# Fixed program order on SyncE and GpSimd for the second part of a fused attention and MoE kernel

## The chip, the cores and the metric

One core of a Trainium2 chip runs the program. Five engines work side by side, each through its own instructions in order: TensorE (PE in the profile; PEld is its weight load), VectorE (DVE), ScalarE (ACT), GpSimd (POOL) and SyncE (SP), which computes nothing here and issues DMAs. GpSimd both computes and issues DMAs. An instruction waits on semaphores, and everything behind it on its engine waits with it. The metric is the time of one execution on the device in microseconds, as the median of several runs.

## What is computed

Eight batches of eight heads, 576 positions, head size 64. Attention looks back over a window of 128 positions, with a bias that falls with distance (ALiBi). Its output, laid out as 4608 tokens of 512, goes through two dense layers with a Swish between them.

```python
def _attn_ref(q, k, v):                       # (8, 8, 576, 64), float32
    scores = scale * np.matmul(q, k.transpose(0, 1, 3, 2))
    mask = (rel >= 0) & (rel < 128)
    scores = np.where(mask, scores + slopes * -np.abs(rel), -1000000000.0)
    attn = np.exp(scores - max); attn = attn / (sum + 1e-09)
    return np.matmul(attn, v)
...
x = attn_out.transpose(0, 2, 1, 3).reshape(4608, 512)
h = x @ w_in                                  # (512, 2048)
g = h * (1.0 / (1.0 + np.exp(-beta * h)))
return g @ w_out                              # (2048, 512)
```

## The kernel before

**Tiles and stages.** A batch has 5 blocks of positions (4 of 128 and one of 64: `NQB = 5`, `ROWS`). Tokens are taken 512 at a time through the dense layers: 9 groups (`NTG`), so a batch is 1.125 groups. `XT` holds the transposed attention output of three groups as a ring.

The steps of attention for batch b:

- Loads of q and k. For batches 0 to 2 by pairs of heads (`load_pair`, L109, `load_tail`), for batches 3 to 7 by blocks (`load_qk`): SyncE loads float32 rows into an `fst` buffer (13 of them; line 95 in `load_rows`), GpSimd casts them to bfloat16 into a `bst` buffer (8 of them; line 126).
- Loads of v (`load_v`). For batches 0 to 2 a SyncE load into `fst` and a GpSimd cast (line 137); for batches 3 to 7 one DMA issued from GpSimd that casts on the way (line 132). There are two `VS` buffers, used by turns.
- Transposes of q and k into `qkT` (two buffers, by turns). For batches 0 to 2 on PE (`TP`, `TT`), for batches 3 to 7 by two DMA transposes per block issued from SyncE (`TD`, line 245), ten in a batch.
- `SC(b, m, p)`: scores of a pair of heads for one half of the key blocks (PE, line 273), exponentials (ACT, line 286) and a mask (DVE, line 290). `sps`, its PSUM tile, is single from batch 2 on.
- `PV(b, qb, g)`: weights times v for one block and four heads (PE, lines 313 and 317), a reciprocal and a multiplication on DVE (lines 322 and 323) that write `xn`.
- `X(b, qb)`: `xn` transposed into `XT`. For batches 0 to 2 on PE; for batches 3 to 7 a DMA transpose issued from SyncE (line 337).

The steps of the dense layers for token group g:

- `HS(g, j)`, j from 0 to 15: four matmuls 128x128 by 128x512 (line 358), tanh on ACT (line 363), one DVE operation (line 364). It reads all of the group's `XT`.
- `OS(g, i, n)`: four matmuls of the second layer (line 374). After every fourth `OS`, ACT writes an `osb` tile (6 buffers, line 380), and a DMA stores it (line 382): issued from GpSimd, for the last group from SyncE.

**Order.** PE's order is written out by hand (`manual_schedule` for PE): `spread` deals a list of attention steps between the dense steps, called items here. H group 1 is pure: 16 `HS` with no attention between them. Then group 1 (`os(0)` and half of `os(1)` with batch 2's attention, 24 items), group 2 (`hs(2)` and the rest of `os(1)`, 24 items), and groups 3 to 8 (`hs(g)` and `os(g - 1)` by turns, 32 items), each with the attention up to the last `X` that the next group's `HS` reads (`end`). For group 2 that is X of batch 3, block 2.

The order on SyncE, GpSimd, ACT and DVE is not the program's: a scheduler sets it when the program is built, from priorities and its own estimate of when an instruction can start. `ahead` only deals loads, casts and DMA transposes of the next batch among the attention steps in the program's text. On the chip each engine then keeps the scheduler's order.

Of the kernel before, what the change touches and what calls it, by code (L numbers as in the profile page):

```python
# [11 lines left out]
BF16 = mybir.dt.bfloat16  # L12
F32 = mybir.dt.float32
P = 128
# [3 lines left out]
def kernel(  # L18
# [10 lines left out]
    nc = tc.nc  # L29
    B, H, S, D = q.shape  # L30
# [8 lines left out]
    NTE = 3  # L39
    LA = 4  # L40
    LM = P * LA
    NQB = 5
    ROWS = [P, P, P, P, 64]
    NDM = DM // P
    NFF = DFF // P
    TOKG = 512
    NTG = T // TOKG
# [8 lines left out]
    NPE = 2  # L56
# [35 lines left out]
    def load_rows(src, b, sb):  # L92
        rows = ROWS[sb]
        f = fst_pool.tile([P, H, D], F32, name="fst", tag="fst")
        nc.sync.dma_start(  # L95
            out=f[0:rows],
            in_=src[b, :, P * sb : P * sb + rows, :].rearrange("h p d -> p h d"),
        )
        return f[0:rows]
# [21 lines left out]
            )  # L121

    def load_qk(b, sb):
        t = bst_pool.tile([P, 2, H, D], BF16, name="bst", tag="bst")
        for i, src in enumerate((q, k)):
            c = nc.gpsimd.tensor_copy(out=t[0 : ROWS[sb], i], in_=load_rows(src, b, sb))  # L126
        staged[b, sb] = t
        return c

    def load_v(b, sb):  # L130
        if b >= NTE:
            nc.gpsimd.dma_start(  # L132
                out=VS[b % 2][0 : ROWS[sb], sb, :, 0:D],
                in_=v[b, :, P * sb : P * sb + ROWS[sb], :].rearrange("h p d -> p h d"),
            )
            return
        return nc.gpsimd.tensor_copy(
            out=VS[b % 2][0 : ROWS[sb], sb, :, 0:D], in_=load_rows(v, b, sb)
        )
# [102 lines left out]
    def TD(b, sb):  # L242
        src = staged.pop((b, sb))
        for i in range(2):
            nc.sync.dma_start_transpose(  # L245
                out=QK[b % 2][:, i, :, P * sb : P * sb + ROWS[sb]],
                in_=src[0 : ROWS[sb], i].rearrange("r h d -> r (h d)"),
            )
# [119 lines left out]
    def OS(g, i, n):  # L368
        gT = gts[g]
        if n == 0:  # L370
            opss[g, i] = psum_o.tile([P, DM], F32, name="ops", tag="ops")
        ops_ = opss[g, i]
        for j in range(4 * n, 4 * n + 4):
            nc.tensor.matmul(  # L374
                ops_[:], lhsT=gT[:, j, i * P : i * P + P], rhs=W2[:, j, :],
                start=(j == 0), stop=(j == NFF - 1),
            )
        if n == 3:
            osb = osb_pool.tile([P, DM], F32, name="osb", tag="osb")
            nc.scalar.mul(osb[:], ops_[:], 0.5)  # L380
            row0 = g * TOKG + i * P
            (nc.sync if g == NTG - 1 else nc.gpsimd).dma_start(out=out[row0 : row0 + P, :], in_=osb[:])  # L382


    def spread(moe, todo, lead=0, tail=3):
        done, n = 0, len(moe)
        for i, it in enumerate(moe):
            it()
            to = len(todo) * (i + 1 - lead) // (n - lead - tail)
            while done < min(len(todo), to):  # L390
                todo[done]()
                done += 1

    def sc(b, m, p):
        return lambda: SC(b, m, p)

    def pv(b, qb, g):
        return lambda: PV(b, qb, g)

    def x(b, qb):  # L400
        f = lambda: X(b, qb)
        at[b, qb] = f
        return f

    at = {}


    def ahead(b, m, r):
        td = [lambda c=c, sb=sb: TD(c, sb) for c, sb in (
            ((b, 3), (b, 4)) if m == 0 else ((b + 1, 0), (b + 1, 1), (b + 1, 2)))]  # L410
        qk = [lambda sb=sb: load_qk(b + 1, sb) for sb in ((0, 1, 2), (3, 4))[m]]
        vs = [lambda sb=sb: load_v(b + m, sb) for sb in ((2, 3, 4), (0, 1))[m]]
        ops = vs if m == 0 else []
        if b + 1 < B:
            ops = td + (vs + qk if m == 0 else qk + vs)
        elif m == 0:
            ops = td + vs
        n, k, out = len(r), 0, []
        for i, f in enumerate(r):
            out.append(f)  # L420
            while k < len(ops) and k * n <= i * len(ops):
                out.append(ops[k])
                k += 1
        return out + ops[k:]

    def by_pair(b):
        return [
            lambda: TP(b, 0), lambda: TP(b, 1), sc(b, 0, 0), lambda: TT(b), sc(b, 0, 1),
            lambda: TP(b, 2), sc(b, 1, 0), lambda: TP(b, 3), sc(b, 1, 1), pv(b, 0, 0), sc(b, 0, 2),
            pv(b, 1, 0), sc(b, 1, 2), pv(b, 2, 0), sc(b, 0, 3), pv(b, 3, 0), sc(b, 1, 3),  # L430
            pv(b, 4, 0), pv(b, 0, 1), pv(b, 1, 1), x(b, 0), pv(b, 2, 1), x(b, 1), pv(b, 3, 1),
            x(b, 2), pv(b, 4, 1), x(b, 3), x(b, 4),
        ]

    def by_block(b):

        e = b - 1
        r = [pv(e, 2, 1), pv(e, 3, 1), x(e, 2), sc(b, 0, 0), x(e, 3), pv(e, 4, 1), sc(b, 0, 1),
             x(e, 4)] if e >= NTE else [sc(b, 0, 0), sc(b, 0, 1)]
        r += [sc(b, 0, 2), pv(b, 0, 0), sc(b, 0, 3), pv(b, 1, 0)]  # L440
        t = [
            pv(b, 0, 1), sc(b, 1, 0), x(b, 0), pv(b, 1, 1), sc(b, 1, 1), x(b, 1),
            sc(b, 1, 2), pv(b, 2, 0), sc(b, 1, 3), pv(b, 3, 0), pv(b, 4, 0),
        ]
        return ahead(b, 0, r) + ahead(b, 1, t)

    with tc.manual_schedule(engines={mybir.EngineType.PE}):

# [64 lines left out]
        def hs(g):  # L513
            return [lambda j=j: HS(g, j) for j in range(NFF)]

        def os(g):
            return [lambda n=n: OS(g, n // 4, n % 4) for n in range(NFF)]


        spread(hs(0), by_pair(1), 3, 0)  # L520
        for sb in range(NQB):
            load_v(2, sb)
        for sb in (0, 1, 2):
            load_qk(3, sb)
        for it in hs(1):
            it()
        for f in ahead(2, 1, [lambda: None]):
            f()
        o1 = os(1)
        spread(os(0) + o1[0:8], by_pair(2))  # L530
        todo = sum((by_block(b) for b in range(NTE, B)), [])
        todo += [pv(B - 1, 2, 1), pv(B - 1, 3, 1), x(B - 1, 2), pv(B - 1, 4, 1), x(B - 1, 3),
                 x(B - 1, 4)]
        done = 0
        for g in range(2, NTG):
            moe = hs(g)
            if g == 2:
                moe = sum((moe[2 * n : 2 * n + 2] + [o1[8 + n]] for n in range(8)), [])
            else:
                moe = sum(([a, c] for a, c in zip(moe, os(g - 1))), [])  # L540
            end = len(todo)
            if g + 1 < NTG:
                b, r = divmod(TOKG * (g + 2) - 1, S)
                end = todo.index(at[b, r // P]) + 1
            spread(moe, todo[done:end], 0, 3 if g == 2 else 6)
            done = end
        for it in os(NTG - 1):
            it()


# [28 lines left out]
```

## Time and profile before

| | |
|---|---|
| median of 3 runs | 381.88 us (381.2 to 382.83) |
| profiled execution, whole | 382.14 us |
| profiled execution, span from first to last instruction | 380.3 us |
| PE busy | 322.1 us, 85% |
| ACT busy | 211.1 us, 56% |
| DVE busy | 195.0 us, 51% |
| GpSimd busy | 105.2 us, 28% |
| HBM read and written | 36.71 and 9.44 MB |

Times in the rows are microseconds from the span's start unless marked ns. "SPq" is SyncE's queue, which issues DMAs; a DMA's "landing" is the time from its issue to the arrival of its data. Idle time of an engine stands with the releaser that ended it. The clock column tells the granted clock of PE as a share of 2.4 GHz.

### The profile page before, as it was taken

How to read it: one execution, taken by the hardware profiler on the slowest of the kernel's cores; microseconds unless marked ns; L12 is line 12 of the kernel's file. 1: busy time of each engine (PE TensorE's matmuls, PEld its weight loads, DVE VectorE, ACT ScalarE, POOL GpSimd, SP SyncE). 2: the span in 40 equal slices, each digit the busy share in tenths (PEclk: the TensorE clock that was granted, in tenths of full speed). 3: DMA queues.
4: the chain of work that ended last, by engine and by line, in shares of the span. 5: the costliest groups of instructions: out<-in, count | busy, mean ns of one | idle time of the engine just before them, and what ended most of it. 6: DMA issues, size and time to landing. Idle time of an engine off the chain costs nothing.

```text
span 380.3 us, 6165 instructions
## 1 busy us (share of the span) xinstructions
PE 322.1 (85%) x2236; PEld 153.4 (40%) x2279; DVE 195.0 (51%) x421; ACT 211.1 (56%) x407; POOL 105.2 (28%) x173
## 2 busy tenths in 40 slices
PE   6988988998989900019999999999998999999996
PEld 2454454444534400004444444544453445444442
DVE  6477577866457800004655665656575647434310
ACT  4655756577188700006777687677667666444421
POOL 6736461812460644142030401130000010001000
PEclk9899999999999955559999999999999999999999
DMA  8899999998999998999371985492111111201012
GB/s 203 199 216 242 245 228 193 199 157 147 207 233 135 189 240 150 190 147 135 71 119 43 125 111 84 85 144 51 41 42 50 43 41 50 69 29 55 28 58 83
DMA packets 138494, 48.26 MB, mean 127 GB/s; under 512 B 125648, under 2 KB 135904, under 8 KB 138464
## 3 DMA queue, kind: packets, MB, share of 16 engines
q1 hardware_dynamic: 108208, 32.33, 46.4%
q0 software_dynamic: 30224, 15.54, 25.4%
q8 instruction: 18, 0.29, 0.4%
q14 instruction: 12, 0.10, 0.1%
q10 hardware_dynamic: 32, 0.01, 0.0%
HBM read 36.71 MB, written 9.44 MB: 121 GB/s over the span
## 4 chain that ended last, share of the span: by engine, by line
PE 56%; DMA 22%; SPq 10%; ACT 4%; POOL 3%; issue 3%; DVE 2%; POOLq 0%
PE ops L374 28%; PE hps L358 22%; DMA fst<-in_k_dram 10%; DMA fst<-in_v_dram 7%; SPq L245 4%; SPq L95 3%; PE sps L273 3%; ACT pt L286 3%; SPq L109 2%; PE pv L317 2%; DMA W<-in_moe_w_in_dram 1%; POOL bst L126 1%; DMA qkT<-bst 1%; PE pv L313 1%; DMA XT<-xn 1%
## 5 line engine op out<-in xcount | busy, mean ns | idle before, releaser
L358 PE MATMUL hps<-XT,W 128*128 128x512 bf16 x556 | 143.6, 381 | 38.4 <-DMA XT<-xn 37.2
L363 ACT ACTIVATE sig<-hps,beta_h 128x512 bf16<-128x512 f32 x144 | 99.5, 693 | 110.1 <-PE hps L358 100.1
L364 DVE SCALAR_TENSOR_TENSOR gT<-sig,hps 128x512 bf16<-128x512 bf16 x144 | 98.2, 684 | 101.5 <-ACT sig L363 100.9
L374 PE MATMUL ops<-W,gT 128*128 128x512 bf16 x557 | 142.8, 380 | 1.0 <-issue 0.2
L358 PEld LDWEIGHTS <-W 128*128 128x128 bf16 x576 | 51.8, 98 | 94.6 <-DMA XT<-xn 37.7
L286 ACT ACTIVATE pt<-sps,bias 128x256 bf16<-128x256 f32 (+1 forms) x192 | 75.2, 478 | 16.1 <-PE sps L273 16.1
L374 PEld LDWEIGHTS <-gT 128*128 128x128 bf16 x576 | 52.6, 98 | 58.1 <-issue 3.4
L382 POOL DMA_DIRECT2D out_dram<-osb x32 | 17.8, 555 | 127.5 <-ACT osb L380 127.5
L290 DVE TENSOR_TENSOR pt<-pt,mask 128x1024 bf16<-128x1024 bf16 x48 | 33.9, 707 | 33.2 <-ACT pt L286 33.1
L126 POOL CAST bst<-fst 128x512 bf16<-128x512 f32 (+1 forms) x50 | 30.7, 624 | 64.4 <-DMA fst<-in_k_dram 31.1
L380 ACT ACTIVATE osb<-ops 128x512 f32<-128x512 f32 x36 | 21.7, 603 | 25.8 <-PE ops L374 25.7
L323 DVE TENSOR_TENSOR xn<-pv,zs 128x256 bf16<-128x256 f32 (+1 forms) x80 | 33.4, 420 | 2.1
L132 POOL DMA_DIRECT2D vs<-in_v_dram x25 | 21.3, 853 | 33.7 <-PE pv L317 32.1
L317 PE MATMUL pv<-vs,pt 128*128 128x65 bf16 x320 | 28.6, 193 | 1.4 <-DVE pt L290 1.4
L273 PE MATMUL sps<-qkT 64*128 64x256 bf16 (+2 forms) x320 | 25.4, 253 | 4.4 <-ACT pt L286 3.9
L317 PEld LDWEIGHTS <-pt 128*128 128x128 bf16 x320 | 21.6, 97 | 11.1 <-DVE pt L290 1.8
L322 DVE RECIPROCAL zs<-pv 128x4 f32<-128x4 f32 (+1 forms) x80 | 13.9, 176 | 21.8 <-PE pv L317 21.2
L313 PE MATMUL pv<-vs,pt 128*128 128x65 bf16 x256 | 23.9, 193 | 0.8 <-DVE xn L323 0.5
L273 PEld LDWEIGHTS <-qkT 64*128 64x128 bf16 x320 | 11.1, 94 | 31.9 <-issue 31.1
L313 PEld LDWEIGHTS <-pt 128*128 128x128 bf16 x256 | 19.7, 98 | 8.1 <-DVE xn L323 1.7
L281 ACT ACTIVATE pt<-sps 128x1024 bf16<-128x1024 f32 x16 | 16.0, 1027 | 9.6 <-PE sps L273 9.2
L113 POOL CAST bst<-fst 128x512 bf16<-128x512 f32 x24 | 14.7, 622 | 11.6 <-DMA fst<-in_q_dram 6.1
(45 smaller groups left out, 107.5 us busy)
## 6 DMA issues: line engine op xcount, KB each, us to landing
fst<-in_q_dram SPq DMA_DIRECT2D x32, 256.0 KB, 5.5
fst<-in_k_dram SPq DMA_DIRECT2D x32, 256.0 KB, 5.7
out_dram<-osb POOLq DMA_DIRECT2D x32, 256.0 KB, 2.7
fst<-in_v_dram SPq DMA_DIRECT2D x12, 256.0 KB, 7.9
vs<-in_v_dram POOLq DMA_DIRECT2D x20, 128.0 KB, 4.8
W<-in_moe_w_in_dram POOLq DMA_DIRECT2D x4, 512.0 KB, 7.7
W<-in_moe_w_out_dram POOLq DMA_DIRECT2D x4, 512.0 KB, 15.0
fst<-in_q_dram SPq DMA_DIRECT2D x8, 128.0 KB, 5.9
```

Source lines behind the costliest of these rows:

```text
L126: c = nc.gpsimd.tensor_copy(out=t[0 : ROWS[sb], i], in_=load_rows(src, b, sb))
L273: nc.tensor.matmul(o, lhsT=qk[64 * e : 64 * e + 64, 1, p, P * kb : P * kb + P], rhs=qk[64 * e : 64 * e + 64, 0, p, P * kb : P * kb + nq], ...
L286: nc.scalar.activation(out=pt[:, e, cols], in_=sps[:, e, cols], func=ACTF.Exp, scale=qscale, bias=bias[:, half, h : h + 1],)
L290: nc.vector.tensor_tensor(out=pt[:], in0=pt[:], in1=masks[m][:].rearrange("p (o c) -> p o c", o=1).broadcast_to([P, 2, 512]), op=ALU.mult,)
L313: nc.tensor.matmul(pv[:, hl, 0 : D + 1], lhsT=weights(b, qb - 1, h, 1), rhs=vs[:, qb - 1, h, 0 : D + 1], start=True, stop=False,)
L317: nc.tensor.matmul(pv[:, hl, 0 : D + 1], lhsT=weights(b, qb, h, 0), rhs=vs[:, qb, h, 0 : D + 1], start=qb == 0, stop=True,)
L323: nc.vector.tensor_tensor(out=xn[0:nq, 4 * g : 4 * g + 4, :], in0=pv[0:nq, :, 0:D], in1=zs[0:nq].broadcast_to([nq, 4, D]), op=ALU.mult,)
L358: nc.tensor.matmul(hps[:], lhsT=W1[:, c, bass.ts(j, P)], rhs=XT[:, c, c0 : c0 + TOKG], start=(c == 0), stop=(c == NDM - 1),)
L363: nc.scalar.activation(out=sig[:], in_=hps[:], func=ACTF.Tanh, scale=beta_h[:, j : j + 1])
L364: nc.vector.scalar_tensor_tensor(out=gts[g][:, j, :], in0=sig[:], scalar=1.0, in1=hps[:], op0=ALU.add, op1=ALU.mult)
L374: nc.tensor.matmul(ops_[:], lhsT=gT[:, j, i * P : i * P + P], rhs=W2[:, j, :], start=(j == 0), stop=(j == NFF - 1),)
L380: nc.scalar.mul(osb[:], ops_[:], 0.5)
```

## The change

From batch 2's v loads on, SyncE and GpSimd too keep the order in which the program is written. `merge` gives every load, cast, DMA transpose and v load of batches 3 to 7 a position among the attention steps (loads 25 steps ahead of the batch's first step, the cast 3.5 and the DMA transpose 6.5 steps behind the load), and puts each X of these batches 2.5 steps behind its place in the list. `load_qk` starts both loads and returns the casts as a function of their own. `load_v` uses the casting DMA from batch 2 on instead of batch 3. Stores are held back: `flush`, called before every dense item, lets a store go at the third item after it was made. `ahead` is gone; group 2 leaves 6 items at its end without attention instead of 3.

```diff
     def load_qk(b, sb):
-        t = bst_pool.tile([P, 2, H, D], BF16, name="bst", tag="bst")
-        for i, src in enumerate((q, k)):
-            c = nc.gpsimd.tensor_copy(out=t[0 : ROWS[sb], i], in_=load_rows(src, b, sb))
-        staged[b, sb] = t
-        return c
+        fs = [load_rows(src, b, sb) for src in (q, k)]
+
+        def cast():
+            t = bst_pool.tile([P, 2, H, D], BF16, name="bst", tag="bst")
+            for i, f in enumerate(fs):
+                nc.gpsimd.tensor_copy(out=t[0 : ROWS[sb], i], in_=f)
+            staged[b, sb] = t
+
+        return cast
 
     def load_v(b, sb):
-        if b >= NTE:
+        if b >= NPE:
             nc.gpsimd.dma_start(
...
-            (nc.sync if g == NTG - 1 else nc.gpsimd).dma_start(out=out[row0 : row0 + P, :], in_=osb[:])
-
+            last = g == NTG - 1
+
+            def store():
+                (nc.sync if last else nc.gpsimd).dma_start(
+                    out=out[row0 : row0 + P, :], in_=osb[:]
+                )
+
+            if last:
+                store()
+            else:
+                stores.append([2, store])
+
+
+    stores = []
+
+    def flush():
+        for e in list(stores):
+            e[0] -= 1
+            if e[0] < 0:
+                e[1]()
+                stores.remove(e)
 
     def spread(moe, todo, lead=0, tail=3):
         done, n = 0, len(moe)
         for i, it in enumerate(moe):
+            flush()
             it()
...
     def x(b, qb):
         f = lambda: X(b, qb)
         at[b, qb] = f
+        if b >= NTE:
+            lazy.append(f)
         return f
...
+    def merge(steps, first):
+        jobs = []
+        for b in range(NTE, B):
+            for sb in range(NQB):
+                casts = []
+                t0 = first[b] - 25 + 4.6 * sb
+                jobs.append((t0, lambda b=b, sb=sb, c=casts: c.append(load_qk(b, sb))))
+                jobs.append((t0 + 3.5, lambda c=casts: c.pop()()))
+                jobs.append((t0 + 6.5, lambda b=b, sb=sb: TD(b, sb)))
+                jobs.append((first[b] - 16 + 3 * sb, lambda b=b, sb=sb: load_v(b, sb)))
+        for i, f in enumerate(steps):
+            if f in lazy:
+                jobs.append((i + 2.5, f))
+        jobs.sort(key=lambda j: j[0])
+        out = []
+        for i, f in enumerate(steps):
+            while jobs and jobs[0][0] <= i:
+                out.append(jobs.pop(0)[1])
+            if f not in lazy:
+                out.append(f)
+        return out + [j[1] for j in jobs]
...
         spread(hs(0), by_pair(1), 3, 0)
-        for sb in range(NQB):
-            load_v(2, sb)
-        for sb in (0, 1, 2):
-            load_qk(3, sb)
-        for it in hs(1):
-            it()
-        for f in ahead(2, 1, [lambda: None]):
-            f()
-        o1 = os(1)
-        spread(os(0) + o1[0:8], by_pair(2))
-        todo = sum((by_block(b) for b in range(NTE, B)), [])
...
+        steps, first = by_pair(2), {}
+        for b in range(NTE, B):
+            first[b] = len(steps)
+            steps += by_block(b)
+        steps += [pv(B - 1, 2, 1), pv(B - 1, 3, 1), x(B - 1, 2), pv(B - 1, 4, 1), x(B - 1, 3),
+                  x(B - 1, 4)]
+        with tc.manual_schedule(engines={mybir.EngineType.SP, mybir.EngineType.Pool}):
+            for sb in range(NQB):
+                load_v(2, sb)
+            for it in hs(1):
+                it()
+            todo, o1, done = merge(steps, first), os(1), 0
+            for g in range(1, NTG):
+                if g == 1:
+                    moe = os(0) + o1[0:8]
+                    end = todo.index(at[2, NQB - 1]) + 1
+                elif g == 2:
+                    moe = hs(2)
+                    moe = sum((moe[2 * n : 2 * n + 2] + [o1[8 + n]] for n in range(8)), [])
+                else:
+                    moe = sum(([a, c] for a, c in zip(hs(g), os(g - 1))), [])
+                if g > 1:
+                    end = len(todo)
+                    if g + 1 < NTG:
+                        b, r = divmod(TOKG * (g + 2) - 1, S)
+                        end = todo.index(at[b, r // P]) + 1
+                spread(moe, todo[done:end], 0, 3 if g == 1 else 6)
+                done = end
+            while stores:
+                flush()
+            for it in os(NTG - 1):
+                it()
```

## Rows read from the trace of the kernel before

**Rows 1.** The page's slices: the span in 40 parts, busy or clock in tenths.

```profile
PE   6988988998989900019999999999998999999996
PEclk9899999999999955559999999999999999999999
```

**Rows 2.** Stages: window, its length; busy us (instructions) by engine, clock, DMA share, GB/s.

```profile
72.10:104.20 32.10, 30.08 (x264) 15.90 (x268) 19.82 (x44) 15.94 (x39) 12.29 (x20) 1.00 1.20 171
104.20:132.60 28.40, 26.32 (x197) 12.25 (x199) 19.86 (x42) 23.10 (x50) 13.12 (x21) 1.00 1.22 188
132.60:169.80 37.20, 0.05 (x1) 0.00 (x0) 0.63 (x1) 0.60 (x1) 14.59 (x24) 0.53 1.19 182
169.80:200.00 30.20, 29.84 (x174) 13.18 (x179) 15.98 (x30) 19.78 (x42) 7.50 (x12) 0.95 0.67 110
```

**Rows 3.** Waits from 122 to 172: who waited for whom, total, times, longest.

```profile
PE hps L358 <- DMA XT<-xn: 37.2, 1, 37.2
```

**Rows 4.** DVE in order of time: start, duration, what it wrote.

```profile
116.87 0.42 DVE L323 TENSOR_TENSOR xn<-pv,zs 128x256 bf16<-128x256 f32 x1
...
120.86 0.42 DVE L323 TENSOR_TENSOR xn<-pv,zs 128x256 bf16<-128x256 f32 x1
...
130.62 0.42 DVE L323 TENSOR_TENSOR xn<-pv,zs 128x256 bf16<-128x256 f32 x1
```

**Rows 5.** SyncE's queue in order of time: start, time over all xcount issues, what.

```profile
48.67 18.23 SPq L95 DMA_DIRECT2D fst<-in_v_dram  x5
...
107.69 15.16 SPq L245 DMA_TRANSPOSE qkT<-bst  x10
...
139.80 5.69 SPq L245 DMA_TRANSPOSE qkT<-bst  x4
...
155.17 8.97 SPq L245 DMA_TRANSPOSE qkT<-bst  x6
...
165.49 3.53 SPq L337 DMA_TRANSPOSE XT<-xn  x2
```

**Rows 6.** GpSimd in order of time; in brackets its idle time before, and what ended it.

```profile
126.55 0.62 POOL L126 CAST bst<-fst 128x512 bf16<-128x512 f32 x1 [11.53 <-DMA fst<-in_k_dram]
...
161.99 0.61 POOL L126 CAST bst<-fst 128x512 bf16<-128x512 f32 x1 [7.08 <-DMA qkT<-bst]
```

**Rows 7.** The first 3.2 us behind the hole as a stage; twelve matmuls in the chain.

```profile
169.80:173.00 3.20, 3.16 (x9) 1.24 (x10) 0.51 (x1) 0.69 (x1) 0.44 (x1) 0.57 0.97 219
...
101.78 2.59 PE ops L374 x12
```

**Rows 8.** ACT in order of time (an `osb`, one SC); the page's group of store issues.

```profile
104.41 0.60 ACT L380 ACTIVATE osb<-ops 128x512 f32<-128x512 f32 x1 [3.55 <-PE ops L374]
...
123.17 1.57 ACT L286 ACTIVATE pt<-sps,bias 128x320 bf16<-128x320 f32 x4
...
L382 POOL DMA_DIRECT2D out_dram<-osb x32 | 17.8, 555 | 127.5 <-ACT osb L380 127.5
```

**Rows 9.** Issues by line over the span: duration in ns, least, median, most.

```profile
L95 SPq DMA_DIRECT2D fst<-in_q_dram x28: 527/682/2162, 2.9 to 171.3; - x28
...
L245 SPq DMA_TRANSPOSE qkT<-bst x50: 1187/1220/2699, 74.5 to 248.5; - x50
...
L337 SPq DMA_TRANSPOSE XT<-xn x26: 1171/1216/2475, 146.8 to 328.2; - x26
...
L132 POOL DMA_DIRECT2D vs<-in_v_dram x25: 692/889/912, 68.7 to 253.3; - x25
```

**Rows 10.** Landing: L95 at 104 to 174, at 49 to 104; L337 to 174, all.

```profile
DMA to landing us min/median/max: 3.1/5.3/8.3
...
DMA to landing us min/median/max: 3.2/5.3/17.3
...
DMA to landing us min/median/max: 2.5/4.0/5.8
...
XT<-xn SPq DMA_TRANSPOSE x26, 3.1
```

More of the change, by code (lines that the diff above doesn't have):

```diff
@@ L402, in x @@
         at[b, qb] = f
-        return f
[L405 to L424, printed above, removed]
+        if b >= NTE:
+            lazy.append(f)
+        return f
+    at, lazy = {}, []
+    def merge(steps, first):
[19 more added lines that the diff above has]
+        return out + [j[1] for j in jobs]
     def by_pair(b):
@@ L439, in by_block @@
              x(e, 4)] if e >= NTE else [sc(b, 0, 0), sc(b, 0, 1)]
-        r += [sc(b, 0, 2), pv(b, 0, 0), sc(b, 0, 3), pv(b, 1, 0)]
-        t = [
+        return r + [
+            sc(b, 0, 2), pv(b, 0, 0), sc(b, 0, 3), pv(b, 1, 0),
             pv(b, 0, 1), sc(b, 1, 0), x(b, 0), pv(b, 1, 1), sc(b, 1, 1), x(b, 1),
@@ L444, in by_block @@
         ]
-        return ahead(b, 0, r) + ahead(b, 1, t)
     with tc.manual_schedule(engines={mybir.EngineType.PE}):
@@ L520 @@
         spread(hs(0), by_pair(1), 3, 0)
-        for sb in range(NQB):
-            load_v(2, sb)
-        for sb in (0, 1, 2):
-            load_qk(3, sb)
-        for it in hs(1):
-            it()
-        for f in ahead(2, 1, [lambda: None]):
-            f()
-        o1 = os(1)
-        spread(os(0) + o1[0:8], by_pair(2))
-        todo = sum((by_block(b) for b in range(NTE, B)), [])
-        todo += [pv(B - 1, 2, 1), pv(B - 1, 3, 1), x(B - 1, 2), pv(B - 1, 4, 1), x(B - 1, 3),
-                 x(B - 1, 4)]
@@ L534 @@
[L534 to L546, printed above, removed]
@@ L547 @@
-        for it in os(NTG - 1):
-            it()
+        steps, first = by_pair(2), {}
[30 more added lines that the diff above has]
+                it()
```

## The prediction

> **What bounds the kernel now.** First the 40 slices: PE is at 9 or 8 tenths nearly everywhere, at 0 in four slices near the middle, and there alone its clock falls [rows 1]. The stage table puts edges on it: from 132.6 to 169.8 us PE is busy 0.05 of 37.2 us, with 26.32 of 28.4 us before and 29.84 of 30.2 us after [rows 2]. So the kernel is PE-bound with one hole. The waits name its end: one wait of 37.2 us of `hps` (the first product of H group 3) for the DMA `XT<-xn` [rows 3], the DMA transpose X of batch 3. Was its input late? No: the last `xn` that it needs, block 2 of batch 3, is written by DVE at 130.62 + 0.42 = 131.0 us [rows 4]. The transpose is issued at 165.49 us [rows 5], 34.5 us later. In between SyncE worked off what the scheduler had put ahead of it: q and k loads for later batches and ten `qkT<-bst` transposes (4 from 139.80, 6 from 155.17) [rows 5]. Transposes come ten to a batch; the ten from 107.69 are batch 4's, so these are batch 5's, which nothing on PE wants before group 4. One of GpSimd's casts waited 7.08 us for such a transpose to give its buffer back, another 11.53 us for a load standing behind ten transposes [rows 6]. So the hole is queue order: an urgent 1.2 us issue behind work for two groups later.
>
> **The change, part by part.** I wrote out both program orders from the lists of the code; step names follow (L load pair, C cast pair, TD transpose pair, V, X, ST store; L51 is batch 5, block 1).
>
> (a) *X gets a place.* After the change X32, which H group 3 waits for, stands on SyncE behind L42 to L44, TD41 to TD44, X30, X31, L50, L51 and TD50; of batch 5's ten transposes only the two of TD50 remain ahead of it, of batch 5's loads four. The hole of 37.2 us goes, and with it a slow start: the granted clock of the hole is 0.53, half of full (1.2 of 2.4 GHz) for nearly all of it [rows 2], and in PE's first 3.2 us of work behind it the clock is 0.57 [rows 7]: 3.2 x 0.43 = 1.4 us lost. Gain 38.6 us.
>
> What is late next is X32 itself. Its new chain starts at the `xn` of block 1, at 120.86 us before [rows 4]. By the new lists four of the group's matmul items stand later than it instead of before it; at four matmuls of 0.216 us (12 in 2.59 us [rows 7]), 0.86 us an item, that is 3.4 us earlier, so ready at 120.86 + 0.42 - 3.4 = 117.9 us. Is SyncE free by then? Issue prices are 0.68 us a load, 1.22 us a transpose [rows 9]. L42 stands right behind TD34, as I place it at about 102 us, and lands 5.3 us later [rows 10], by 108; the store ahead of C42 has its `osb` at 104.41 + 0.60 [rows 8], no later; C42 to 109, TD42 to 111.6, L44 to 113. X30's `xn` came at 117.29 before [rows 4] and comes three items, 2.6 us, earlier: 114.7; X30 to 115.9, TD43 to 118.4. Then X31 to 119.6, L50 to 121.0, its k half landing 5.3 us after its issue at 120.3 [rows 10], 125.6; cast 0.62 us [rows 6] to 126.2; TD44 and L51 fit in that wait; TD50 to 128.7; X32 lands 3.1 to 4.0 us later (3.1 is the median of all, 4.0 that of the crowded stretch [rows 10]): 131.8 to 132.7. PE gets there at about 132.6 + 0.4 for sc400, which now also lies in this group. So the new wait is near 0. Its bounds: with 8.3 us of landing, the longest in this stretch, 2 us; with 17.3 us, the longest of the stretch before it [rows 10], 11 to 12 us, plus the 1.4 us of a new clock dip. Below nothing it can't go: PE is in program order there. I take 1 us, near the median row, because SyncE can also be late for TD43.
>
> (b) *Loads and casts are separate, with loads 25 steps ahead.* L, C and TD stand 3.5 and 3 steps apart, about 1.4 us a step (group 2 has 20 in 28.4 us [rows 2]), so 5 us and 4 us, against 5.3 us of landing: a TD seldom waits long. GpSimd's casts now stand behind stores in order (C31 behind the first store, C32 behind the second), so they follow PE's pace. That costs nothing as long as TD32 is done when group 2 opens at 104.2 us; it stands behind the second store: 8 items of 32.1 / 24 = 1.34 us [rows 2] from 72.1 us, then some 5 us for that store, V, cast and issue, so about 88 us. If that cover went, sc300 would wait, and PE with it.
>
> (c) *v of batch 2 becomes a casting load on GpSimd.* Removed: 5 SyncE loads, whose issues held SyncE for 18.23 us from 48.67 us [rows 5]; 5 casts of 0.62 us; 5 of 13 `fst` buffers in use. Added: 5 GpSimd issues of 0.89 us [rows 9], 4.5 us, right behind batch 2's pair casts. First reader is batch 2's first PV, behind six items of group 1, which opens at 72.1 us; H group 1, pure matmul, covers them. On the path 0; batch 3's loads can start some 15 us earlier, which feeds (b).
> All 25 issues of this kind in the trace take 0.692 to 0.912 us [rows 9], those of group 2 among them, where DVE is busy 19.86 of 28.4 us [rows 2]; so DVE's work costs them nothing that shows. A rule of the Trainium skill speaks against (c) all the same, and the trace does not bear it out: the page SBUF — State Buffer, section SBUF: two separate sides, says that a DMA issued from GpSimd can't get its descriptors written while VectorE holds the port that both share, and the section behind it gives 620 ns alone against about 3100 ns beside a VectorE copy. By these figures, an estimate, the five V of batch 4 would come 12.4 us later and the time be about 357 us.
>
> (d) *Stores stand three items later in the queue.* The 0.56 us store issues used to hold GpSimd for 127.5 us in all, waiting for `osb` [rows 8]; now a cast or V standing in the two items between goes first. Nothing waits for a store but a buffer, six of them, and one store comes every 7 to 8 us. On the path 0.
>
> (e) *PE's own order.* Each group's share of attention steps is now counted in a list that holds the jobs too, and group 2 leaves 6 instead of 3 items free of attention at its end. Per group PE's steps hardly move (group 2: 17 to 18, group 3: 11 to 12, group 7: 10 to 8), but in group 2 sc301 and sc302 become neighbours. One sc costs ACT about four ACTIVATEs, 1.57 us [rows 8], and ACT is busy 23.10 of 28.4 us there [rows 2]; `sps` is single, so a neighbour waits about 1 us. I take 1 us; bounds 0 and 4 us (group 2's last three attention items at ACT's pace).
>
> **Sum.** The profiled execution took 382.14 us for a span of 380.3 us; the median of three is 381.88. 382.14 - 37.2 - 1.4 + 1.0 (X32) + 1.0 (sc) = 345.5 us. The rest of the span is taken as it was: 29.84 of 30.2 us busy directly behind the hole [rows 2], so what PE does from there on has no more to give.
>
> **Rivals.**
> *Residual wait, 353 to 358 us (0.16).* L50's landing or a late TD43 puts X32 8 to 12.4 us late, clock dip included: 345.5 + 8 to + 12.4. For: X32 stands right behind TD50, whose load is issued only after X31. Against: in the stretch itself no landing exceeds 8.3 us [rows 10].
> *Pacing, 350 to 354 us (0.12).* Uneven steps make sc after sc wait for ACT, 1 us in each of five attention groups, or the casts behind stores make one early TD late by 3 to 5 us. For: ACT at 81% in group 2 [rows 2]. Against: only one pair of neighbours in the new order.
> *Slower than before, 385 to 410 us (0.04).* Fixed order on two in-order queues that wait on one another becomes the pace: at each of the six ends of groups 2 to 7 an X stands behind a TD, its cast, its load. It decides when each of the six ends loses over 38.6 / 6 = 6.4 us, that is, when loads land in over 12 to 13 us every time; at 17.3 us, six times 11 us give 343.5 + 66 = 410. Against: median 5.3 [rows 10], and from group 3 on the load stands two to three X further ahead.
> *It does not do what it says, 382 us (0.02).* The hole would have to come from the DMA engines. Against: once issued, X landed in about 4 us [rows 10].
> *Below 342 us (0.03).* Less load traffic also removes part of the 2.08 us of PE idle in group 2.
> *GpSimd's issues wait for DVE, 348 us (0.01).* DVE runs 42 instructions in 19.86 us in group 2 [rows 2], 0.47 us each; if each V of batch 4 waits one out, C44 and C50 come 5 x 0.47 = 2.4 us late, and so does X32. Against: the narrow spread of the 25 issues [rows 9].
>
> **How the numbers follow.** Forecast 0.62, 342 to 350 us, predicted 345.5. With the residual wait and the pacing that is 0.90, up to 358; the range 342 to 357 leaves out the lowest case, the tail of the residual wait and the two cases at 382 and above, under 0.2. A measurement here tells 0.5% (1.9 us) from no change: faster 0.94, same 0.02, slower 0.04.
>
> **What would show it.** Right: no 37 us wait for `XT<-xn`; PEclk without the run of fives; X of batch 3, block 2 issued within about 2 us of 128 us; H group 3 beginning near 133 us; v of batch 2 on line L132's counterpart, 30 issues; the last stage of pure matmuls as long as before. Wrong: several waits of 3 us or more for `XT<-xn` or `qkT<-bst` at ends of groups (slower rival), idle PE before `sps` (pacing), GpSimd issues of well over 0.9 us (waiting for DVE), or a hole of the old size at another place.

## The result, and the profile after

The changed kernel takes 351.96 us, median of four runs (348.44 to 353.64), against 382.01 us before: a ratio of 0.920 (95% interval 0.912 to 0.929), so 30 us or 8% faster. The prediction said 345.5 us, in a range of 342 to 357. The profiled execution took 353.56 us for a span of 351.7. Medians below leave out the executions that count as slow: 660.75 us of e1, 478.39 us of e8, 351.64 and 352.48 us of e12.

The page of the kernel after, its slices (busy or clock in tenths, as in [rows 1]):

```profile
PE   6998968898999888999999999999999999999995
PEclk9699998999999899999999999999999999999999
```

The empty slices (three at 0 and one at 1 in [rows 1], where the prediction read four zeros) and the run of fives are gone. What is left in the clock are small dips: the second slice, which stands as an 8 in [rows 1] too, the seventh, and the fourteenth. The waits of the kernel after (who waited for whom: total us, times, longest):

```profile
PE pv L321 <- POOL vs L141: 4.2, 4, 2.6
PE sps L277 <- ACT pt L290: 3.8, 6, 1.7
```

No wait of PE for `XT<-xn` stands in that list; [rows 3] was 37.2 us. (Lines after the loads' helper have moved: `hps` is L362, `ops` L378, `osb` L384, the store L389, v's casting load L136, v's cast L141, TD L249, X L341.)

To see where time went, the span is cut at three `osb` tiles on ACT, which hold the same work in every kernel here: the sixth (end of group 1), the eighth (end of group 2) and the last from group 8. ACT's timeline, first before, then after:

```profile
132.69 0.60 ACT L380 ACTIVATE osb<-ops 128x512 f32<-128x512 f32 x1 [0.17 <-PE ops L374]
...
376.73 0.60 ACT L380 ACTIVATE osb<-ops 128x512 f32<-128x512 f32 x1 [2.86 <-PE ops L374]
```

```profile
110.35 0.60 ACT L384 ACTIVATE osb<-ops 128x512 f32<-128x512 f32 x1 [3.55 <-PE ops L378]
...
143.38 0.60 ACT L384 ACTIVATE osb<-ops 128x512 f32<-128x512 f32 x1 [0.18 <-PE ops L378]
...
347.80 0.60 ACT L384 ACTIVATE osb<-ops 128x512 f32<-128x512 f32 x1 [2.86 <-PE ops L378]
```

The sixth of before is in [rows 8], at 104.41. The same cut for all kernels of the study follows (us). The columns are differences of such starts and come from the one profiled execution of each kernel; the time is the median of its runs. An execution takes about 1.8 us more than its span, and the profiled one lies up to 2.3 us from the median (after, e7, e8, e11, e12). e3, e4 and e5 have one run each.

| kernel | what it is | to 6th `osb` | 6th to 8th | 8th to last | span | time |
|---|---|---|---|---|---|---|
| before | the kernel before | 104.4 | 28.3 | 244.0 | 380.3 | 382.0 |
| after | the kernel after | 110.4 | 33.0 | 204.4 | 351.7 | 352.0 |
| e1 | after, with v of batch 2 tied behind a cast | 104.6 | 32.7 | 204.4 | 345.6 | 347.4 |
| e2 | after, with v of batch 2 staged as before | 105.5 | 31.3 | 205.4 | 345.7 | 347.6 |
| e3 | before, with the casting load for v of batch 2 | 107.9 | 28.3 | 246.4 | 386.5 | 388.2 |
| e4 | e1, only SyncE in fixed order | 105.4 | 31.4 | 204.6 | 345.2 | 347.0 |
| e5 | e1, only GpSimd in fixed order | 106.5 | 31.5 | 218.1 | 359.9 | 361.7 |
| e6 | before, its own text order fixed | 104.1 | 28.7 | 218.8 | 355.1 | 357.7 |
| e7 | e1, 3 items free at the end of group 2 | 105.3 | 29.2 | 207.4 | 345.8 | 349.4 |
| e8 | e1, lists dealt by PE's steps | 106.1 | 30.6 | 206.3 | 346.8 | 346.4 |
| e9 | e1, each X two places earlier | 105.1 | 30.6 | 209.1 | 348.7 | 351.0 |
| e10 | e1, stores not held back | 104.0 | 31.3 | 214.0 | 353.3 | 355.5 |
| e11 | e9 and e7 together | 105.8 | 29.6 | 211.2 | 350.4 | 350.0 |
| e12 | e8, e9 and e7 together | 105.8 | 30.0 | 207.8 | 347.6 | 347.3 |

After against before: the front loses 5.9 us, group 2 loses 4.7, the rest gains 39.6 (the hole of 37.2 and 2.4 more), the last few us lose 0.3: 28.6 us of span. So the experiments had three questions: what was lost in the front, what in group 2, and which part of the change gained the rest.

### The profile page after: what moved, and what is told of

It reads as the page before. It is cut to its first block, busy times and chain, and to the rows that moved or that the text cites. A ratio compares the mean times of both kernels' runs of the same rounds, so it can differ in the third digit from the quotient of the medians.

```text
span 351.7 us, 6171 instructions
## 1 busy us (share of the span) xinstructions
PE 328.2 (93%) x2279; PEld 154.7 (44%) x2279; DVE 197.6 (56%) x421; ACT 211.0 (60%) x407; POOL 106.0 (30%) x173
## 4 chain that ended last, share of the span: by engine, by line
PE 53%; DMA 17%; issue 10%; SPq 8%; POOL 6%; DVE 3%; ACT 3%; POOLq 0%
PE ops L378 24%; PE hps L362 24%; DMA fst<-in_q_dram 8%; DMA fst<-in_v_dram 5%; SPq L95 3%; POOL bst L129 3%; PE sps L277 3%; SPq L249 2%; SPq L109 2%; ACT pt L290 2%; DMA fst<-in_k_dram 2%; DMA W<-in_moe_w_in_dram 2%; PE pv L321 1%; POOL vs L136 1%; PE pv L317 1%
## 5 line engine op out<-in xcount | busy, mean ns | idle before, releaser
L362 PE MATMUL hps<-XT,W 128*128 128x512 bf16 x576 | 146.3, 383 | 0.3 <-DVE gT L368 0.3
L378 PE MATMUL ops<-W,gT 128*128 128x512 bf16 x576 | 145.2, 380 | 0.0
L362 PEld LDWEIGHTS <-W 128*128 128x128 bf16 x576 | 52.5, 98 | 59.0 <-issue 4.8
L378 PEld LDWEIGHTS <-gT 128*128 128x128 bf16 x576 | 52.3, 98 | 57.9 <-issue 2.4
L389 POOL DMA_DIRECT2D out_dram<-osb x32 | 17.9, 559 | 174.3 <-ACT osb L384 174.3
L294 DVE TENSOR_TENSOR pt<-pt,mask 128x1024 bf16<-128x1024 bf16 x48 | 35.8, 746 | 24.1 <-ACT pt L290 24.1
L384 ACT ACTIVATE osb<-ops 128x512 f32<-128x512 f32 x36 | 21.7, 603 | 26.3 <-PE ops L378 26.3
L321 PE MATMUL pv<-vs,pt 128*128 128x65 bf16 x320 | 29.3, 195 | 6.4 <-POOL vs L141 4.2
L317 PE MATMUL pv<-vs,pt 128*128 128x65 bf16 x256 | 24.7, 194 | 1.3 <-DVE xn L327 1.0
L136 POOL DMA_DIRECT2D vs<-in_v_dram x30 | 25.5, 854 | 0.5 <-issue 0.4
L230 DVE COPY qkT<-tps 128x512 bf16<-128x512 bf16 x24 | 15.6, 685 | 4.8 <-PE tps L226 4.8
```

Of the source, the lines that this page charges most:

```text
L136: nc.gpsimd.dma_start(out=VS[b % 2][0 : ROWS[sb], sb, :, 0:D], in_=v[b, :, P * sb : P * sb + ROWS[sb], :].rearrange("h p d -> p h d"),)
L294: nc.vector.tensor_tensor(out=pt[:], in0=pt[:], in1=masks[m][:].rearrange("p (o c) -> p o c", o=1).broadcast_to([P, 2, 512]), op=ALU.mult,)
L317: nc.tensor.matmul(pv[:, hl, 0 : D + 1], lhsT=weights(b, qb - 1, h, 1), rhs=vs[:, qb - 1, h, 0 : D + 1], start=True, stop=False,)
L321: nc.tensor.matmul(pv[:, hl, 0 : D + 1], lhsT=weights(b, qb, h, 0), rhs=vs[:, qb, h, 0 : D + 1], start=qb == 0, stop=True,)
L362: nc.tensor.matmul(hps[:], lhsT=W1[:, c, bass.ts(j, P)], rhs=XT[:, c, c0 : c0 + TOKG], start=(c == 0), stop=(c == NDM - 1),)
L378: nc.tensor.matmul(ops_[:], lhsT=gT[:, j, i * P : i * P + P], rhs=W2[:, j, :], start=(j == 0), stop=(j == NFF - 1),)
```

## The experiments

**The front: v of batch 2.** In the kernel after, PE waits for casts of batch 1's v. GpSimd's timeline (start, duration; in brackets idle time before), one wait of PE, a stage behind it in the columns of [rows 2], and the landing of SyncE's block loads from 20 to 49 us (least, median, most):

```profile
27.14 0.89 POOL L136 DMA_DIRECT2D vs<-in_v_dram  x1
...
40.86 0.70 POOL L136 DMA_DIRECT2D vs<-in_v_dram  x1
...
50.58 0.61 POOL L141 CAST vs<-fst 128x512 bf16<-128x512 f32 x1 [4.12 <-DMA fst<-in_v_dram]
...
51.24 0.19 PE L321 MATMUL pv<-vs,pt 128*128 128x65 bf16 x1 [2.61 <-POOL vs L141]
...
52.00:56.00 4.00, 3.75 (x27) 1.85 (x26) 1.53 (x6) 1.71 (x2) 4.00 (x7) 0.59 1.06 189
...
DMA to landing us min/median/max: 4.8/11.0/13.4
```

Batch 2's five casting loads, which the code issues behind `hs(0)`, were issued from 27 to 41 us, in the middle of the first loads: the fixed order of a block orders the instructions of that block among themselves, and the scheduler placed these five ahead of others that stand before the block. In the same stretch of before, SyncE's loads land in 6.1/7.9/16.6 us. Besides the 4.2 us of waits, the clock is at 0.59 in the four us behind the longest: 4 x 0.41 = 1.6 us more.

e1 keeps the casting loads and makes them come after the last pair cast of batch 2:

```diff
-            load_pair(2, p)
+            c = load_pair(2, p)
...
+            with tc.issue_after(c.ins):
                 for sb in range(NQB):
                     load_v(2, sb)
```

> The changed kernel, with the five v loads of batch 2 queued on GpSimd behind batch 2's last pair cast, where the prediction had placed them; in the changed kernel they are issued at 27 to 41 us, among the loads of batch 1. Theory A (they take DMA time from batch 1's v, for which PE then waits): the four waits of PV for the casts of v, 4.2 us in all, go; the first second-layer matmul of group 1, 77.5 us in the changed kernel and 72.1 before, is back at 72 to 73; the time falls by about 5 us from 352 to 345 to 348. Rival B (the front is late for another reason, a slow clock early in the program or another order on ACT and DVE): group 1 still begins at 76 to 78 us, time 350 to 354.

347.35 us (346.85 to 348.21), ratio 0.909 (0.907 to 0.911). The five loads now hold GpSimd for 4.20 us from 57.82 us, no wait of PE for `vs` is left, and the front is back at 104.6: theory A.

e2 is the kernel after with batch 2's v staged as before:

```diff
     def load_v(b, sb):
-        if b >= NPE:
+        if b >= NTE:
```

> The changed kernel, but v of batch 2 goes the old way: five loads from SyncE into float32 buffers and five casts on GpSimd, in fixed order. Theory A: the front is as before (group 1 begins at 72 to 73 us), the time 345 to 348; SyncE's first load of batch 3 comes some 15 us later, which the 30 us up to group 2 still cover. Rival B: 350 to 354. A third outcome, group 2 begins with PE waiting for a transpose of batch 3: then the casting load is needed for what follows, about 350.

347.61 us (347.24 to 348.82), ratio 0.910 (0.908 to 0.912). So the casting load of batch 2 isn't needed for the gain, and as it is placed it costs some 4.4 us by the medians (351.96 - 347.61). How much of that each execution lost is not shown: the kernel after spreads by 5 us, its fastest execution (348.44 us) lies within 1 us of e2's median, and the trace is of a long one.

e3 is the opposite: the kernel before with that one line changed, one run.

```diff
     def load_v(b, sb):
-        if b >= NTE:
+        if b >= NPE:
```

> The kernel before, with one thing of the change: v of batch 2 loaded by the casting DMA; all order left to the scheduler. Theory A: the five loads come out early here too, so PV of batch 1 waits for casts of v and group 1 begins at 76 to 78 us instead of 72.1; the hole in front of H group 3, whose end SyncE's queue sets, swallows it or grows with it: 378 to 388 us. Rival B: group 1 begins at 72 to 73 us, time as before within 3 us.

388.24 us; group 1 begins at 75.59 us and ends 3.5 us later than before, less than theory A's 76 to 78, and the hole stays:

```profile
PE hps L358 <- DMA XT<-xn: 38.3, 1, 38.3
...
PE pv L317 <- POOL vs L137: 2.2, 2, 1.4
```

So a loss in the front goes with these five loads, in the old order as in the new. That they lengthen the landing of the others fits the medians of that stretch: 11.0 us in after and 9.7 in e3, where the five loads run there, against 7.9 in before, 7.7 in e1 and 6.7 in e2, where they don't. It wasn't measured apart.

**The gain: order, or places?** e6 takes the kernel before, its text from H group 1 on unchanged, and only fixes that order on SyncE and GpSimd:

```diff
+        with tc.manual_schedule(engines={mybir.EngineType.SP, mybir.EngineType.Pool}):
             for sb in range(NQB):
                 load_v(2, sb)
...
```

> The kernel before, with its own text order made the order of SyncE and GpSimd from batch 2's v loads on; no new positions, stores not held back, loads and casts in one step, v of batch 2 the old way. If fixing the order is what removes the hole, the wait of H group 3 for the transposed attention output falls from 37.2 us to under 8 us and the time is 343 to 355. If it takes the new positions, because casts behind unready loads hold stores and DMA transposes, a hole of 15 us or more stays, at this or other places, and the time is above 360.

357.71 us (355.3 to 358.65), ratio 0.935 (0.931 to 0.940): the wait falls under 8 us as in the first case, but the time lies between the two bands. The old text, merely obeyed, already gives 24 us of the gain. What it lacks against e1 is two waits at ends of groups, which end at 136.89 and 208.55 us, and the clock, at 0.50 in the four us behind each (2 us each); its group 2 is 4 us shorter than e1's:

```profile
PE hps L358 <- issue: 4.2, 1, 4.2
...
PE hps L358 <- DMA XT<-xn: 3.7, 1, 3.7
```

e4 and e5 are e1 with only one of the two engines fixed, one run each:

```diff
-        with tc.manual_schedule(engines={mybir.EngineType.SP, mybir.EngineType.Pool}):
+        with tc.manual_schedule(engines={mybir.EngineType.SP}):       # e4
+        with tc.manual_schedule(engines={mybir.EngineType.Pool}):     # e5
```

> As e1_v2_late, but only SyncE keeps the program's order; GpSimd's is left to the scheduler again. Theory: the hole was SyncE's order alone, so it stays away (no wait for the transposed attention output over 5 us) and the time is 345 to 352. Rival (the two queues wait on one another, so both must be fixed): casts come in another order than the transposes that wait for them, waits of 5 us or more, time over 355.

> As e1_v2_late, but only GpSimd keeps the program's order; SyncE's is left to the scheduler. Theory: the transposes of the attention output again stand behind loads and transposes of later batches, and a hole of 20 us or more stays: 365 to 385 us. Rival (GpSimd's order, casts behind stores, paces the loads and so also clears SyncE's queue): hole under 8 us, 345 to 356.

e4: 347.0 us, no wait for `XT`. e5: 361.71 us, with one wait in front of H group 3:

```profile
148.95 1.89 PE L362 MATMUL hps<-XT,W 128*128 128x512 bf16 x4 [11.05 <-DMA XT<-xn]
```

With the new places, SyncE's order alone is enough. With GpSimd's alone the hole is 11 us instead of 37, which neither theory had. What took the 26 us is open: no run has the new places with neither engine fixed, so the new places may by themselves have given the scheduler a better order for SyncE. Another way, only argued: GpSimd's casts stand behind stores, a cast frees the `fst` buffer of the next load, and so SyncE can't run as far ahead.

**The stores held back.** e10 is e1 with each store issued in its place:

```diff
-            if last:
-                store()
-            else:
-                stores.append([2, store])
+            store()
```

> As e1_v2_late, but each store is put in GpSimd's order where it is made, not three items later. The prediction put holding the stores back at 0 on the path. If that is right, the time stays at 347 to 349. If casts that now stand behind a store not yet ready come later by up to two items, 1.7 us and more, the transposes behind them and with them X of batch 3, block 2 come later too: a wait in front of H group 3 of 1 to 4 us, 349 to 352.

355.46 us (355.13 to 355.8), ratio 0.928 (0.922 to 0.934): 8 us slower than e1, more than expected. GpSimd and SyncE at the start of group 1, first e1, then e10, with e10's wait in front of H group 3 last:

```profile
64.99 0.61 POOL L129 CAST bst<-fst 128x512 bf16<-128x512 f32 x1 [2.97 <-PE hps L362]
...
65.63 5.17 SPq L249 DMA_TRANSPOSE qkT<-bst  x2
...
80.59 0.59 POOL L389 DMA_DIRECT2D out_dram<-osb  x1 [12.18 <-ACT osb L384]
```

```profile
80.21 0.58 POOL L389 DMA_DIRECT2D out_dram<-osb  x1 [16.52 <-ACT osb L384]
80.78 2.28 POOL L129 CAST bst<-fst 128x512 bf16<-128x512 f32 x4
...
81.44 3.84 SPq L249 DMA_TRANSPOSE qkT<-bst  x2
...
142.45 1.86 PE L362 MATMUL hps<-XT,W 128*128 128x512 bf16 x4 [7.14 <-DMA qkT<-bst]
```

Without the delay the first store stands ahead of the first two pairs of casts, and GpSimd sits in front of it for 16.5 us. The first TD comes 15.8 us later, the loads behind it too, and that lateness isn't made up: X30 leaves at 124.41 us against 118.46 in e1, X32 at 139.92 against 132.49. The profile puts the wait down to a `qkT` transpose; X32, issued behind it, lands after 2.4 us, at 142.3, where the wait ends too. The clock is at 0.50 in the four us behind the wait.

**Group 2.** In the kernel after, `sc` steps that are now close together wait longer for ACT, and behind the first wait the granted clock falls. PE's timeline, first before, then after with a stage of four us in the columns of [rows 2], and last PE's waits for ACT and DVE from 100 to 150 us:

```profile
107.47 0.39 PE L273 MATMUL sps<-qkT 64*128 64x256 bf16 x4 [0.94 <-ACT pt L286]
...
109.52 0.39 PE L273 MATMUL sps<-qkT 64*128 64x256 bf16 x4 [0.69 <-ACT pt L286]
```

```profile
113.41 0.40 PE L277 MATMUL sps<-qkT 64*128 64x256 bf16 x4
115.46 0.40 PE L277 MATMUL sps<-qkT 64*128 64x256 bf16 x4 [1.66 <-ACT pt L290]
...
128.00 0.40 PE L277 MATMUL sps<-qkT 64*128 64x256 bf16 x6 [0.94 <-ACT pt L290]
...
116.35:120.35 4.00, 4.00 (x19) 1.32 (x17) 2.57 (x5) 3.25 (x9) 1.70 (x3) 0.57 1.69 171
...
PE sps L277 <- ACT pt L290: 2.6, 2, 1.7
...
PE pv L321 <- DVE pt L294: 0.9, 2, 0.5
```

At 0.57 of full speed, near the lower of the two levels, four us lose 4 x 0.43 = 1.7 us. e7 gives group 2 its old tail of three items free of attention:

```diff
-                spread(moe, todo[done:end], 0, 3 if g == 1 else 6)
+                spread(moe, todo[done:end], 0, 3 if g <= 2 else 6)
```

> As e1_v2_late, with one number of the change undone: group 2 again leaves 3 items free of attention at its end, not 6. In e1_v2_late group 2 takes 32.7 us against 28.3 before, with PE waiting 1.66 us between two neighbouring SC steps and a clock of 0.57 for 4 us behind that. Theory C (group 2 is longer because its attention is packed into 18 items): the SC steps get one or two items between them, the 1.66 us wait falls under 0.8 us, the clock does not fall, group 2 takes 29 to 30.5 us, and the time falls by 2 to 3.5 us to 344 to 346; a wait of 0 to 2 us for the transposed output of batch 3, block 2 can appear in front of H group 3. Rival D (ACT or DMA traffic, not the packing): group 2 stays at 32 us or more and the time within 1 us of e1_v2_late.

Group 2 shrinks to 29.2 us, its longest `sc` wait to 0.69 us, the clock stays at 1.00; but the time is 349.44 us (347.53 to 350.76), ratio 0.915 (0.912 to 0.918), by the medians 2 us above e1, where 344 to 346 was expected. The profiled execution is the fastest of the four and as long as e1's (spans 345.8 and 345.6); what the others lost beyond it is in no trace. In it, the gain comes back as a wait at the next step. SyncE, then PE, of e7:

```profile
130.79 3.64 SPq L249 DMA_TRANSPOSE qkT<-bst  x2
134.53 2.54 SPq L341 DMA_TRANSPOSE XT<-xn  x2
...
137.21 1.02 PE L362 MATMUL hps<-XT,W 128*128 128x512 bf16 x4 [2.77 <-issue]
```

The profile names no releaser for the 2.77 us; X32 leaves only at 134.53, right behind TD50, although its `xn` was written by 131.06. The transposes X there land 2.6 to 4.0 us after their issue, and 134.53 + 2.6 is the end of the wait. e11 bears out that it is X32.

e8 deals the lists by PE steps alone, so that a load or cast takes no attention step's place:

```diff
+        cost = [0 if f in light else 1 for f in todo]
...
-            to = len(todo) * (i + 1 - lead) // (n - lead - tail)
-            while done < min(len(todo), to):
+            to = sum(cost) * (i + 1 - lead) // (n - lead - tail)
+            while done < len(todo) and spent + cost[done] <= to:
```

> As e1_v2_late, 6 items free again, but each group deals its list by PE's steps alone: loads, casts, transposes and v loads no longer count. So no two SC steps are neighbours, yet group 2 still holds 18 attention steps in 18 items. Theory C (packing): the waits of SC for ACT are spread, 0.7 to 1 us each at three places, group 2 stays at 31 to 32.5 us; if it is the one wait of 1.66 us that lets the clock fall, the clock stays up and the time falls by about 2 us to 345 to 346.5. Rival D: no change within 1 us.

346.42 us (346.0 to 348.55), ratio 0.907 (0.904 to 0.911): the same as e1 within the intervals. Nine `sc` waits of at most 0.94 us stand in place of six of up to 1.66, in all 6.4 us against 3.8. The clock stays at 1.00 in group 2, which takes 30.6 us, but the rest takes 1.9 us more than in e1.

e9 is e1 with X two places earlier among the steps:

```diff
-                jobs.append((i + 2.5, f))
+                jobs.append((i + 0.5, f))
```

> As e1_v2_late, but each X of batches 3 to 7 stands directly behind the attention step that finishes its input, not 2.5 steps later; X of batch 3, block 2 is then ahead of the transposes of batch 5's first block on SyncE (132.5 us in e1_v2_late, 2 us behind its ready input). Theory E (the two transposes ahead of it set when it can go): X of block 2 is issued within 0.8 us of its xn, about 1.5 to 2 us earlier; with 6 items free behind it this is more cover than PE needs, so the time falls only by what group 2 loses to sc400, which moves to group 3: 345 to 347.5. Rival F (SyncE, now waiting at each X for its input, holds the loads behind it back): waits of PE for transposes or loads of batches 5 to 7, time 349 to 353.

350.98 us (350.22 to 351.86), ratio 0.917 (0.912 to 0.922): slower than e1, against the theory; the time lies in the rival's band. X32 did leave earlier (130.60 us) and group 2 took 30.6 us. But the wait came back at the end of group 4. SyncE, then PE, of e9:

```profile
191.93 4.69 SPq L249 DMA_TRANSPOSE qkT<-bst  x2
196.72 1.22 SPq L341 DMA_TRANSPOSE XT<-xn  x1
...
199.39 2.56 SPq L341 DMA_TRANSPOSE XT<-xn  x2
...
203.84 1.89 PE L362 MATMUL hps<-XT,W 128*128 128x512 bf16 x4 [3.14 <-DMA XT<-xn]
```

In e1 the X51 of this place leaves at 195.72, 3.7 us sooner, and PE doesn't wait. SyncE's rows further back show why, and it is what the rival says: from 171.5 to 176.32 us SyncE issues nothing, because X of batch 4, block 2, now in front, stands there until its `xn` is written (by 176.26). The pair of loads behind it leaves at 177.57, in e1 at 166.95, and the transposes of later blocks follow late, two of them right in front of X50. Only PE feels it at an X and not at a transpose or load. PE also comes sooner, at 200.70 against 202.93 in e1: a group's list ends with its last X, so moving X forward shortens what PE has to do before it needs it. The clock is 0.58 for the 3.6 us behind the wait.

e11 is e9 with e7's tail, e12 is e8 with both edits:

> e9_x_at_once with 3 instead of 6 items free at the end of group 2. In e7_tail3 the looser packing shortened group 2 from 32.7 to 29.2 us, and a wait of 2.8 us in H group 3, which begins as X of batch 3, block 2 is issued, gave it back. Theory E: with X issued about 2 to 3 us earlier that wait falls under 1 us, group 2 stays at 28.5 to 30 us, and the time is 343.5 to 346, 2 to 4 us under e1_v2_late. Rival G (the wait of 2.8 us came from something else than this X): it stays, and the time is 347 to 350.

> e11_x_tail3 with the lists dealt by PE's steps alone, as in e8_pe_steps. If even spacing adds to what e11_x_tail3 gives: 342.5 to 345. If group 2 is then at ACT's pace anyway (23 to 24 us of ACT work in about 28), the same as e11_x_tail3 within 1 us.

e11: 350.04 us (349.31 to 352.7), ratio 0.916 (0.912 to 0.920), against the 343.5 to 346 that theory E gave. X32 leaves 27.5 us after the sixth `osb` (at 133.27) instead of e7's 29.3, and the wait in front of H group 3 falls from 2.77 to 0.41 us, so it was X32's, as the theory said; the time is lost again at the wait in front of H group 5, as in e9:

```profile
135.78 1.02 PE L362 MATMUL hps<-XT,W 128*128 128x512 bf16 x4 [0.41 <-issue]
...
205.01 1.04 PE L362 MATMUL hps<-XT,W 128*128 128x512 bf16 x4 [3.98 <-DMA XT<-xn]
```

e12: 347.32 us from two executions, 345.25 and 349.39, ratio 0.907 (0.900 to 0.914), with a wait of 1.28 us in front of H group 5. That is outside 342.5 to 345, and the spread is too wide to say whether it beats e1 or e11.

## Why the prediction was right, and by what it was off

The direction, the mechanism of the gain and the range held; the forecast's own band (342 to 350) missed the median by 2 us. That the range held is in part luck: it was made wide for late transposes and uneven steps, and the largest miss, the front, is in none of its rivals. With the v loads where the prediction had put them (e1), the time is 347.35 us, inside the forecast's band. By its steps, against the profiled execution (353.56 us, 8.1 over the forecast):

**(a) The hole: right.** 37.2 us gone, no hole of any size at another place; the stretch behind group 2 gained 39.6 us where hole and slow start were priced at 38.6. That queue order was the cause is shown by e6 (fixed order alone, 24 us) and e4 (the new places with SyncE alone fixed, all of it).

**(a) X32's time: the chain was mis-sized.** X32 was to be issued near 128 us and H group 3 to begin near 133; both come some 10 us later, at 138.38 and 143.18, and the late front is 5.9 of that. SyncE's timeline after, then the head of the chain in e7 (DVE's `xn` of X30, and X30):

```profile
128.67 1.21 SPq L341 DMA_TRANSPOSE XT<-xn  x1
...
135.38 2.90 SPq L249 DMA_TRANSPOSE qkT<-bst  x2
138.38 3.47 SPq L341 DMA_TRANSPOSE XT<-xn  x2
```

```profile
117.22 0.42 DVE L327 TENSOR_TENSOR xn<-pv,zs 128x256 bf16<-128x256 f32 x1
...
119.13 2.05 SPq L341 DMA_TRANSPOSE XT<-xn  x1
```

The prediction ended TD50 at 128.7, 24.3 us after the sixth `osb`; it ended 27.9 us after it here (138.28 - 110.35) and 29.2 in e7. In e7 the chain's head, X30, had its `xn` 12.4 us after the sixth `osb` instead of 10.3, left 1.5 us later still behind the load pair in front of it, and took 2.05 us instead of 1.22; TD50 took 3.64 instead of 2.44. In the kernel after, PE's own losses in group 2 hid that: no wait. In e2, where the clock doesn't fall, 0.77 us of it shows. With group 2 packed well (e7) it shows as 2.8 us, where 1 was taken and 11 to 12 was the upper bound.

**(b) Loads and casts apart: right, with its cover.** TD32 was put at about 88 us; it is issued at 94.00, which is 88 plus the late front, well before group 2.

**(c) v of batch 2: wrong, and the largest miss in the profiled execution.** Priced 0 on the path; the front lost 5.9 us, of it some 5.4 ahead of group 1 (its first `ops` matmul is at 77.52 us, in [rows 2] the stage opens at 72.1). The step that failed is "right behind batch 2's pair casts": the place was read from the code's text, but the fixed order binds only what stands inside the block. Moved there by e1 the loads cost nothing, as priced (104.6 us to the sixth `osb`, 104.4 before). Issue on GpSimd wasn't the trouble: 30 issues of 692/884/927 ns (least, median, most), against 692/889/912 in [rows 9]. So the rule on GpSimd's descriptors that the prediction weighed (the Trainium skill, SBUF — State Buffer, SBUF: two separate sides) is not borne out after the change either. But that section itself ties the rule to DVE operations in a 2-port mode, such as a float32 copy, which the prediction overlooked; by a later section of the same page of the Trainium skill (Who interferes with whom), copies, casts and tensor_scalar can enter such a mode, while tensor_tensor has none. In group 2 DVE's largest works are the mask and `xn`, both TENSOR_TENSOR, and the `gT` SCALAR_TENSOR_TENSOR, so these rows don't test the rule at its own condition.

**(d) Stores later: right sign, no price.** It was put at nothing, with "nothing waits for a store but a buffer". What waits is every cast behind the store, and through the casts SyncE's TD and loads: 8 us by e10, under the fixed order. The prediction saw the cast going first, and didn't ask what would happen if it did not.

**(e) PE's order: the wait right, what came with it missing.** 1 us for `sc` (and 0.4 for sc400, which never came into the sum) against 4.7 us in group 2. The waits of `sc` there rose by just 1.0 us, from 0.94 + 0.69 to 1.66 + 0.94. Not in the sum were the clock's fall behind the longest (1.7 us), and 1.5 us of short waits of PE for DVE where before has none; the 0.5 us left are near sc400's 0.4. Packing alone isn't worth that, though: e7 takes 3.5 us out of group 2 and gets 2.8 back at X32. The two terms X32 and `sc` share one end (PE waits only for the later of the two chains), and adding them as if apart was wrong in kind.

Sum of the misses in span: 5.4 (front) + 0.5 (group 1) + 2.8 (group 2, over the 2.0 priced for `sc` and X32) - 0.7 (the rest) = 8.0 us.

**The rivals.** The time fell where "pacing" had put it (350 to 354), but that is only partly its mechanism: `sc` waited longer in group 2 and not in five groups (over the whole span its waits for ACT are 3.8 us after and 3.9 before), and the larger loss was the front, which no rival named. The slower rival needed over 6.4 us at each of six ends of groups; the worst kernel with the new places in order (e10) lost 7 us at one.

**Left open.** No variant is shown to be better than e1, e2, e4 (one run) and e8, at 346.4 to 347.6 us some 1.4% below the change as made. Whether some packing reaches 345 us every time, as one execution of e12 did, is not settled. Nor is it settled what GpSimd's fixed order adds, as e4 does without it.

## What to carry to other kernels

Fixing an order by hand binds only the instructions inside the block; look up in the trace when a first, unbound instruction of it really issues, and pin it to something. On an in-order queue price an instruction by what stands behind it: a store that waits for its tile, ahead of a cast, cost 8 us here, and an X behind ten transposes 37. Moving the urgent issue far to the front isn't free either: while it waits for its input, it holds the loads behind it (e9). When an end of a stage is set by two chains, work out both to the same point in time: shortening one only shows the other.

## What the runs showed of the hardware

- The clock can fall behind a very short wait, and not every time. Behind the same 1.66 us wait of PE for ACT, the granted clock was 0.57 for four us in the kernel after and in e1, and 1.00 in e2, e4, e5 and e10. The stage behind the wait, first in e1, then in e2:

```profile
110.56:114.56 4.00, 4.00 (x19) 1.33 (x17) 2.49 (x5) 3.19 (x9) 2.00 (x3) 0.57 1.66 182
```

```profile
110.58:114.58 4.00, 4.00 (x34) 1.85 (x34) 3.11 (x7) 3.57 (x9) 1.18 (x2) 1.00 1.70 214
```

The same four us hold 19 matmuls in the one and 34 in the other. The length of the wait alone doesn't decide either: in the four us behind 2.61 us in the front of the kernel after the clock was 0.59, behind 2.77 us in e7 it was 1.00, and behind 4.2 and 3.7 us in e6 it was 0.50. What does was not found.

- The runs of the kernel after spread by 5 us, and their mean clock doesn't order them: spans of 346.6 us at 0.995, 348.5 at 0.990, 351.7 at 0.981 and 351.9 at 0.990. So a median of few runs of such a kernel is good to some 1%, an estimate from this spread.
- An X that waits for its input holds the DMAs behind it on SyncE: in e9 SyncE issued nothing for 4.8 us (171.5 to 176.32). A store that waits for its tile does the same to casts on GpSimd: 16.5 us in e10.
